# Means and variances of tiles 12 to 15 by ScalarE's accumulators instead of VectorE's statistics

## The chip, the cores and the metric

The kernel runs on one core of one Trainium2 chip. The metric is the time of one execution in device microseconds. The engines are TensorE (PE; its weight loads are PEld), VectorE (DVE), ScalarE (ACT) and GpSimd (POOL). SyncE (SP) issues most of the loads and stores.

## The reference

Two layers, each of an attention block and a gated feed-forward block, both behind a layer norm without weights. The sequence has 2048 rows of 448; there are 16 query heads of 28, and one key and one value head that all share.

```python
def _layernorm(x, axis=-1, eps=1e-5):
    m = jnp.mean(x, axis=axis, keepdims=True)
    v = jnp.var(x, axis=axis, keepdims=True)
    return (x - m) / jnp.sqrt(v + eps)
...
        q = (lambda x, *d: x.transpose(*d))((x @ wq).reshape(B, S, H, Dh), 0, 2, 1, 3)
        k = x @ wk
        v = x @ wv
        scores = jnp.einsum("bhqd,bkd->bhqk", q, k) * (Dh ** -0.5)
        p = _softmax(scores, axis=-1)
        o = jnp.einsum("bhqk,bkd->bhqd", p, v)
...
        g = jnp.einsum("bsd,df->bsf", x, w_gate)
        u = jnp.einsum("bsd,df->bsf", x, w_up)
        h = _sigmoid(g) * u
        return jnp.einsum("bsf,fd->bsd", h, w_down)

    x = A_x
    x = x + _A_ref(_layernorm(x, axis=-1), A_wq, A_wk, A_wv, A_wo)
    x = x + _B_ref(_layernorm(x, axis=-1), B_w_gate, B_w_up, B_w_down)
    x = x + _A_ref(_layernorm(x, axis=-1), A_wq, A_wk, A_wv, A_wo)
    x = x + _B_ref(_layernorm(x, axis=-1), B_w_gate, B_w_up, B_w_down)
```

## The kernel before

The 2048 rows are 16 tiles of 128 rows. Each number that TensorE multiplies is split into two float16 parts, a high one and a low one, and a product of two is three matmuls. Ahead of the main loop stands a prologue of some 90 us. In it each tile of x is loaded (`load_x0`, L900), gets its mean and variance, is normalised (L947 on ScalarE, L949 on VectorE), is cast to its high part (L953), has its low part made (two rows, L958 and L959, on VectorE or GpSimd), is transposed by TensorE in seven pieces (L335) and copied out of PSUM into XT (L337). From XT come the tile's keys and values (`kv`, L352, copied out in the rows L379, L380 and L381) and, by four tiles, the queries (qp, also L352, copied out in L406 and L409). As soon as keys and queries are there, TensorE forms score blocks only for the row maxima (mx, L549), which VectorE reduces (mp, L554). The main loop that follows computes scores (s, L584), their exponentials (L587) and the products with the values (pv, L595), with the feed-forward matmuls in between.

The order of the prologue is written out by hand as the string `SEQ`: each word is a step and its arguments, and the steps are issued in that order, so that on every engine the instructions stand in the order of the words. Some steps defer an instruction until the next step that flushes. `h,n` gives n matmuls on the identity (hot, L916) whose result nobody reads. The words that matter here:

- `s,a,z,how`: statistics of tiles a to z−1 on VectorE, one `bn_stats` (L924) and one `bn_aggr` (L925) a tile. With how = 1 or 2 the reciprocal root follows on GpSimd (`rstd`, eight short rows from L306 to L314 with how = 2)
- `n`, `g`, `l`, `t`, `k`, `c`: norm, high part, low part, transposes, keys, and the transposed keys of one tile
- `qs,c`: square sum of one quarter of the query weights on ScalarE (L109), `qw,c,how`: its split into high and low part (L126 or L135 on ScalarE, then L127 on VectorE, or L136 and L137 on GpSimd)

The step `s,12,16,2` stands behind `k,8`. The tiles' loads are all issued by SP at the start, tiles 12 to 15 last, and each load of SP's queue takes the next of eight semaphores (DMAHW0 to DMAHW7), so it is issued only once the load eight places ahead of it has landed. Buffers of the accumulating passes and of the squares, junx and junq, are three slots in rotation.

Of the kernel before, what the change touches and what calls it, by code (L numbers as in the profile page):

```python
# [8 lines left out]
F32 = mybir.dt.float32  # L9
F16 = mybir.dt.float16  # L10
I32 = mybir.dt.int32
AF = mybir.ActivationFunctionType
OP = mybir.AluOpType
# [6 lines left out]
def interleaved_layers_kernel(ctx: ExitStack, tc: tile.TileContext, x, wq, wk, wv, wo, wg, wu, wd, out, layers=2):  # L20
# [6 lines left out]
    nc = tc.nc  # L27
    _, S, D = x.shape
# [13 lines left out]
    wk1 = ctx.enter_context(tc.tile_pool(name="wk1", bufs=2))  # L42
# [105 lines left out]
    def prep_kv():  # L148
        junk = wk1.tile([128, 4, Dh], F32, tag="xr", name="junk", bufs=4)
        squares(mxa[:, 0:1], rkv[:, 0], junk)  # L150
        squares(mxa[:, 1:2], rkv[:, 1], junk)
        yield from scales(mxa[:, 0:2], 2, pwa[:, 0:2], swa[:, 0:2])
        for i in range(2):
            split(WKV[:, 0, :, i * Dh:(i + 1) * Dh], WKV[:, 1, :, i * Dh:(i + 1) * Dh], rkv[:, i], swa[:, i:i + 1])
# [149 lines left out]
    def rstd(mv, r, n, bias=False):  # L304
        v, y, z, w = (r[:, k, :n] for k in range(4))
        nc.gpsimd.tensor_scalar(v, mv[:, :n, 1], EPS, None, op0=OP.add)  # L306
        nc.gpsimd.tensor_tensor(y, v, mhalf[:, :n], op=OP.pow)
        nc.gpsimd.tensor_tensor(z, y, y, op=OP.mult)
        nc.gpsimd.tensor_tensor(z, z, v, op=OP.mult)
        nc.gpsimd.tensor_scalar(z, z, -1024.0, 3072.0, op0=OP.mult, op1=OP.add)  # L310
        nc.gpsimd.tensor_tensor(w, y, z, op=OP.mult)
        if bias:
            nc.gpsimd.tensor_scalar(z, mv[:, :n, 0], -1.0, None, op0=OP.mult)
            nc.gpsimd.tensor_tensor(z, z, w, op=OP.mult)  # L314
            return [(z[:, i:i + 1], w[:, i:i + 1]) for i in range(n)]
        return [(mv[:, i, 0:1], w[:, i:i + 1]) for i in range(n)]
# [576 lines left out]
    xr0 = {}  # L893
# [8 lines left out]
    hl0, ls0 = {}, {}  # L902
# [69 lines left out]
            pass  # L972
        kv_done(0)

    raw0 = {}
    pkv = prep_kv()
    parts = wk1.tile([128, 4], F32, name="parts", bufs=1)
    pws = scales(mxa[:, 2:3], 1, pwa[:, 2:3], swa[:, 2:3])
# [24 lines left out]
    def first_mx():  # L1003
        nonlocal nmx
        flush()
        while QDONE.get((0, 0), 0) <= nmx % G and QDONE.get((0, 0), 0) < G:
# [1 line left out]
        mxs[0].step()  # L1008
        nmx += 1

    DO = {"s": stats, "r": refine, "n": norm, "g": high, "l": low, "t": turn, "k": keys, "c": keyst, "m": first_mx,
          "h": heat, "a": lambda: next(pkv, None), "qs": qsq, "qx": qsum, "qy": lambda: next(pws), "qw": qsplit,
          "q": queries, "f": lambda a: fill.slice(a * QCH / 100), "p": advance, "e": flush}
    SEQ = (
# [13 lines left out]
    )  # L1028
    for o in SEQ.split():
        a = o.split(",")  # L1030
        DO[a[0]](*map(int, a[1:]))
    for b in range(1, NB):
# [26 lines left out]
    for l in range(layers):  # L1059
# [8 lines left out]
        else:  # L1068
            mx.todo.sort()
            n = sum(a[0] < 4 for a in mx.todo) + 4  # L1070
# [10 lines left out]
        for step in range(U * KT):  # L1081
# [6 lines left out]
            for o in pair[kt % 2]:  # L1088
                if o == "S":
                    scores(l, u, kt, len(P), P)  # L1090
                elif o == "M":
                    if l and step < 3 * KT:
                        n = step in sparse
                    else:
                        n = 1 + (u == 0 and kt in MORE)
                    if not n:
                        mx.visit()
                    for _ in range(n):
                        if not mx.step() and not final and l + 1 in mxs:
                            a = mxs[l + 1].between()  # L1100
# [28 lines left out]
        n = 0  # L1129
        nx = None if final else mxs[l + 1]  # L1130
        while side or pend or (fill.gens if final else not nx.started()):
# [4 lines left out]
            a = None if final else nx.between()  # L1136
            if a:
# [7 lines left out]
                if go:  # L1145
                    nx.step(a)
                    n = 0
# [25 lines left out]
```

## Time and profile before

| what | value |
|---|---|
| median of 3 runs | 2244.06 us (2243.4 to 2244.54) |
| the profiled execution | 2247.71 us |
| its span | 2245.9 us |
| TensorE busy, share of the span | 2195.5 us, 98% |
| VectorE busy | 1643.7 us, 73% |
| ScalarE busy | 1552.8 us, 69% |
| GpSimd busy | 335.9 us, 15% |
| mean granted TensorE clock | 0.995 |

The three runs are without a profile; the profiled execution is one more, and every duration below comes from it. Busy shares are means over the whole span, and a prologue of 90 us is 4% of it, so they say nothing on who waits for whom there; for that the timelines of the engines are read.

### The profile page before, as it was taken

The page shows a single profiled execution, that of the slowest core. Times are in us where ns is not written, and L with a number is a line of the kernel's source. Part 1 is how long each engine was busy: PE and PEld are TensorE (multiplying, and loading weights), DVE is VectorE, ACT ScalarE, POOL GpSimd, SP SyncE. Part 2 cuts the span into 40 slices and gives each one's busy share as a digit, 9 for nine tenths or more (in the row PEclk, how much of TensorE's full clock was granted, in tenths as well). Part 3 has the DMA queues.
Part 4 walks back from the last instruction along what each step waited for, and adds up shares of the span by engine and source line. Part 5 has one row for each costly group of instructions (what it writes and reads, how often), then busy time and mean ns, then how long its engine had stood idle before and what let it go on. Part 6 is the DMA issues. An engine that isn't in the chain of part 4 may idle for free.

```text
span 2245.9 us, 41454 instructions
## 1 busy us (share of the span) xinstructions
PE 2195.5 (98%) x15915; PEld 1030.8 (46%) x15915; DVE 1643.7 (73%) x2905; ACT 1552.8 (69%) x2595; POOL 335.9 (15%) x590
## 2 busy tenths in 40 slices
PE   7998999999999999999999999999999999999999
PEld 3322344444544445454564324445454544445467
DVE  7888888777777787777796557777777777777222
ACT  5698777776667677676614997777676767777741
POOL 5113764101010100101012010000000000000010
PEclk9999999999999999999999999999999999999999
DMA  4333662323313232331441113323231313223233
GB/s 143 106 97 94 197 215 81 106 79 85 112 60 102 64 100 90 97 107 49 119 154 35 36 52 108 80 88 99 67 108 49 100 59 103 76 88 96 75 118 108
DMA packets 203622, 213.28 MB, mean 95 GB/s; under 512 B 135376, under 2 KB 164240, under 8 KB 203424
## 3 DMA queue, kind: packets, MB, share of 16 engines
q1 hardware_dynamic: 198080, 195.78, 29.2%
q0 software_dynamic: 5344, 14.87, 1.9%
q8 instruction: 124, 2.03, 0.4%
q14 instruction: 74, 0.61, 0.1%
HBM read 175.37 MB, written 23.59 MB: 89 GB/s over the span
## 4 chain that ended last, share of the span: by engine, by line
PE 86%; DVE 8%; ACT 2%; issue 1%; DMA 1%; SPq 1%; POOL 0%; DVEq 0%; ACTq 0%; POOLq 0%
PE pv L595 20%; PE s L584 19%; PE up L352 11%; PE dn L784 11%; PE gp L352 11%; PE mx L549 7%; DVE mp L554 6%; PE wo L695 3%; PE qp L352 2%; ACT P L587 1%; DMA wgu<-wgu_d 0%; DMA rq<-in_A_wq_dram 0%; DMA rc<-sums 0%; PE hot L916 0%; DVE sgu L131 0%
## 5 line engine op out<-in xcount | busy, mean ns | idle before, releaser
L587 ACT ACTIVATE P<-s,esc 128x512 f32<-128x512 f32 x2048 | 1297.8, 690 | 474.5 <-PE s L584 462.8
L554 DVE TENSOR_REDUCE mp<-mx 128x1 f32<-128x512 f32 x2048 | 1269.4, 682 | 389.2 <-PE mx L549 385.4
L584 PE MATMUL s<-QS,KK 96*128 96x512 f16 x2048 | 673.8, 381 | 21.3 <-DVE mp L554 14.8
L352 PEld LDWEIGHTS <-wgu 128*128 128x128 f16 x4928 | 467.6, 97 | 182.1 <-issue 42.9
L595 PE MATMUL pv<-P,VV 128*32 128x512 f32 x4096 | 510.7, 602 | 0.0
L352 PE MATMUL gp<-XT,wgu 128*128 128x256 f16 x2464 | 349.2, 272 | 2.4 <-DVE mp L554 1.7
L352 PE MATMUL up<-XT,wgu 128*128 128x256 f16 x2464 | 348.3, 272 | 0.7 <-DVE mp L554 0.7
L784 PE MATMUL dn<-WD,h 128*128 128x448 f16 x1344 | 301.0, 352 | 0.0
L584 PEld LDWEIGHTS <-KK 96*128 96x128 f16 x2048 | 189.7, 97 | 212.5 <-issue 114.5
L595 PEld LDWEIGHTS pv<-P,VV 128*32 128x32 f32 x4096 | 98.7, 108 | 244.6 <-issue 242.6
L549 PE MATMUL mx<-KK,QH 32*128 32x512 f16 x1792 | 185.3, 386 | 3.0 <-DVE mp L554 1.7
L784 PEld LDWEIGHTS <-h 128*128 128x128 f16 x1344 | 126.5, 97 | 129.4 <-issue 14.5
L549 PEld LDWEIGHTS <-QH 32*128 32x128 f16 x1792 | 46.0, 91 | 256.5 <-issue 252.7
L669 POOL TENSOR_TENSOR lb<-pvs,lb 128x512 f32<-128x512 f32 x32 | 41.1, 1284 | 739.1 <-DMA lb<-sums 619.8
L757 ACT ACTIVATE h<-th 128x512 f16<-128x512 f32 x112 | 70.3, 628 | 61.8 <-DVE th L754 61.5
L754 DVE SCALAR_TENSOR_TENSOR th<-th,up 128x512 f32<-128x512 f32 x112 | 76.2, 680 | 48.9 <-PE up L352 42.2
L306 POOL TENSOR_SCALAR rs<-mv 128x1 f32<-128x1 f32 (+1 forms) x50 | 11.2, 225 | 656.6 <-DVE mv L291 573.6
L352 PE MATMUL qp<-XT,WQ 128*128 128x512 f16 x352 | 108.3, 390 | 0.7 <-DVE mp L554 0.4
L746 ACT ACTIVATE th<-gp,gsc 128x512 f32<-128x512 f32 x112 | 76.8, 685 | 32.8 <-PE gp L352 32.6
L758 DVE SCALAR_TENSOR_TENSOR h<-th,h 128x512 f16<-128x512 f32 x112 | 79.9, 713 | 20.8 <-ACT h L757 20.8
L695 PE MATMUL wo<-WO,oT 128*128 128x448 f16 x384 | 89.7, 352 | 0.2 <-ACT P L587 0.2
L352 PEld LDWEIGHTS <-WQ 128*128 128x128 f16 x352 | 32.9, 99 | 54.9 <-issue 28.9
(151 smaller groups left out, 918.1 us busy)
## 6 DMA issues: line engine op xcount, KB each, us to landing
wgu<-wgu_d SPq DMA_DIRECT2D x224, 512.0 KB
QS<-qd SPq DMA_DIRECT2D x384, 32.0 KB
lb<-sums SPq DMA_DIRECT2D x128, 64.0 KB
xr<-in_A_x_dram SPq DMA_DIRECT2D x32, 224.0 KB
qd<-qst POOLq DMA_DIRECT2D x28, 256.0 KB, 2.7
wgu_d<-sgu POOLq DMA_DIRECT2D x14, 512.0 KB, 3.7
x2d<-x SPq DMA_DIRECT2D x16, 224.0 KB
xr<-x2d SPq DMA_DIRECT2D x16, 224.0 KB
```

Source lines behind the costliest of these rows:

```text
L352: nc.tensor.matmul(ps, a, b, start=n == 0, stop=n == 10)
L549: nc.tensor.matmul(ps[h][:, i * w:(i + 1) * w], qh[32 * h:32 * h + 32, g], KK[l][32 * h:32 * h + 32, 1, ka:kz], start=True, stop=True, til ...
L554: nc.vector.tensor_reduce(o, ps[h].rearrange("p (g k) -> p g k", g=n), axis=AX.X, op=OP.max)
L584: nc.tensor.matmul(s, KK[l][0:96, 0, kt * 128:(kt + 1) * 128], QS[l, u][:, g].rearrange("p h n -> p (h n)"), start=True, stop=True)
L587: nc.scalar.activation(p, s, AF.Exp, scale=esc)
L595: nc.tensor.matmul(v[32 * g:32 * g + 32], VV[l][:, kt], P[g], start=kt == 0, stop=kt == KT - 1, tile_position=(0, 32 * g))
L695: nc.tensor.matmul(p, v["oT"][:, a, h * 128:(h + 1) * 128], WO[:, c, h], start=n == 0, stop=n == 11)
L746: defer(lambda: nc.scalar.activation(th, gp.rearrange("p j n -> p (j n)"), AF.Tanh, scale=gsc))
L754: nc.vector.scalar_tensor_tensor(t, th, 1.0, up.rearrange("p j n -> p (j n)"), op0=OP.add, op1=OP.mult)
L757: nc.scalar.activation(h[:, 0], t, AF.Copy, scale=2.0 ** -17)
L758: defer(lambda: nc.vector.scalar_tensor_tensor(h[:, 1], t, 2.0 ** -17, h[:, 0], op0=OP.mult, op1=OP.subtract), 3)
L784: nc.tensor.matmul(p, hs[f // 2][:, a, o:o + 128], WD[:, f, c], start=n == 0, stop=n == 3 * FC - 1)
```

## The change

The words `s,12,16,2` leave `SEQ`, and with them VectorE's four pairs of statistics and one `rstd` chain on GpSimd. In their place stand four words `x,i` (`total`): ScalarE passes over the raw tile and accumulates its sum, and GpSimd multiplies the sum by −1/448. Four words `y,i` (`spread_of`): ScalarE squares the tile with that negative mean as its bias and accumulates the squares. And one word `z,12` (`settle`): GpSimd forms mean and variance of the four tiles from the sums and runs the same `rstd` chain. The new words are dealt between the steps of the first four keys, `z` behind the second pass of tile 15.

```diff
-    raw0 = {}
+    def sm_of(i):
+        a = i // 4 * 4
+        if a not in sm0:
+            sm0[a] = wk1.tile([128, 3, 4], F32, name="sm", bufs=2)
+        return [sm0[a][:, k, i - a:i - a + 1] for k in range(3)]
+
+    def total(i):
+        sm = sm_of(i)
+        junk = wk1.tile([128, D], F32, tag="s2", name="junx", bufs=3)
+        nc.scalar.activation(junk, xr0[i], AF.Identity, accum_out=sm[0])
+        nc.gpsimd.tensor_scalar(sm[1], sm[0], -1.0 / D, None, op0=OP.mult)
+
+    def spread_of(i):
+        sm = sm_of(i)
+        junk = wk1.tile([128, D], F32, tag="s2", name="junx", bufs=3)
+        nc.scalar.activation(junk, xr0[i], AF.Square, bias=sm[1], accum_out=sm[2])
+
+    def settle(a):
+        mv = wk1.tile([128, 4, 2], F32, name="mv", bufs=4)
+        r = wk1.tile([128, 4, 4], F32, name="rs", bufs=4)
+        sm = sm0[a]
+        nc.gpsimd.tensor_scalar(mv[:, :, 0], sm[:, 1], -1.0, None, op0=OP.mult)
+        nc.gpsimd.tensor_scalar(mv[:, :, 1], sm[:, 2], 1.0 / D, None, op0=OP.mult)
+        for j, t in enumerate(rstd(mv, r, 4, True)):
+            ls0[a + j] = t
+
+    sm0, raw0 = {}, {}
...
-        "qs,2 h,2 qs,1 n,2,0 a e g,3,0 t,0,0 l,3,0 t,1,0 qs,0 g,2,0 h,2 l,2,1 k,0 h,3 s,4,8,1 h,5 t,2,1 qx qy "
-        "k,1 c,0,0 k,2 e t,3,1 c,1,0 n,4,0 h,1 qw,0,0 h,5 n,6,0 qw,1,1 h,2 k,3 n,5,0 qw,2,0 h,1 g,4,0 h,2 "
...
-        "s,12,16,2 g,10,0 t,9,0 f,75 c,7,0 m h,2 m n,11,1 h,1 h,3 k,9 l,10,1 n,12,1 h,1 t,10,0 g,11,0 f,110 "
...
+        "qs,2 h,2 qs,1 n,2,0 a e g,3,0 t,0,0 l,3,0 t,1,0 x,12 qs,0 g,2,0 h,2 l,2,1 k,0 x,13 h,3 s,4,8,1 h,5 "
+        "t,2,1 qx qy k,1 c,0,0 x,14 k,2 x,15 e t,3,1 c,1,0 y,12 n,4,0 h,1 qw,0,0 h,5 n,6,0 qw,1,1 h,2 k,3 "
+        "y,13 n,5,0 qw,2,0 h,1 g,4,0 h,2 l,4,0 qw,3,1 g,5,0 y,14 q f,50 l,5,0 t,4,0 c,2,1 y,15 z,12 c,3,1 "
```

On ScalarE, around the square of the last quarter of the query weights (junq) and the first key (ktl, VV), the queue differs so. The tiles are xr_159, 161, 163 and 165 for 12 to 15; in brackets stands whom a row waits for.

```order
 L337 COPY XT_121<-t_258 128x7x128 [waits PE_49]
+L984 ACTIVATE junx,sm<-xr_159 128x448 [waits DMAHW2_49,Activation_49]
 L109 ACTIVATE junq,parts<-rq 128x448 [waits Activation_49]
-L953 CAST hl_279<-xr_136 128x448 [waits DVE_49]
+L953 CAST hl_283<-xr_136 128x448 [waits DVE_49]
 L337 COPY XT_121<-t_269 128x7x128 [waits PE_49]
+L984 ACTIVATE junx,sm<-xr_161 128x448 [waits DMAHW3_49,Activation_49]
 L379 ACTIVATE ktl_111<-kv 128x7x28 [waits PE_49]
 L380 ACTIVATE VV<-kv 128x28
```

Tile 12's total stands ahead of that square and waits for its load, and tile 13's ahead of the first key. The cast is the same on both sides but for a buffer's number.

Some 2 us further in the same queue, from the first transposed keys (KK) to the splits of the query weights (WQ):

```order
 L379 ACTIVATE ktl_112<-kv 128x7x28 [waits PE_49]
 L380 ACTIVATE VV<-kv 128x28
+L984 ACTIVATE junx,sm<-xr_163 128x448 [waits DMAHW4_49,Activation_49]
 L392 COPY KK<-kvt 128x2x128 [waits PE_49]
+L984 ACTIVATE junx,sm<-xr_165 128x448 [waits DMAHW5_49,Activation_49]
 L379 ACTIVATE ktl_111<-kv 128x7x28 [waits DVE_49,PE_49]
 L380 ACTIVATE VV<-kv 128x28
+L990 ACTIVATE junx,sm<-xr_159,sm 128x448 [waits Pool_49]
 L126 ACTIVATE WQ<-rq,swa 128x16x28 [waits DVE_49]
 L135 ACTIVATE WQ<-rq,swa 128x16x28
 L392 COPY KK<-kvt 128x2x128 [waits PE_49]
+L990 ACTIVATE junx,sm<-xr_161,sm 128x448 [waits Activation_49,Pool_49]
```

The totals of tiles 14 and 15 stand ahead of the third key, the square of tile 12 ahead of the first two splits of the query weights, and that of tile 13 ahead of the two that follow.

On SP nothing moves. These are its loads of tiles 6 to 15, xr_147 to xr_165, as they stand in both kernels:

```order
L900 DMA xr_147<-in_A_x_dram 128x448 [waits DMAHW4_49]
L900 DMA xr_149<-in_A_x_dram 128x448 [waits DMAHW5_49]
L900 DMA xr_151<-in_A_x_dram 128x448 [waits DMAHW6_49]
L900 DMA xr_153<-in_A_x_dram 128x448 [waits DMAHW7_49]
L900 DMA xr_155<-in_A_x_dram 128x448 [waits DMAHW0_49]
L900 DMA xr_157<-in_A_x_dram 128x448 [waits DMAHW1_49]
L900 DMA xr_159<-in_A_x_dram 128x448 [waits DMAHW2_49]
L900 DMA xr_161<-in_A_x_dram 128x448 [waits DMAHW3_49]
L900 DMA xr_163<-in_A_x_dram 128x448 [waits DMAHW4_49]
L900 DMA xr_165<-in_A_x_dram 128x448 [waits DMAHW5_49]
```

The load of tile 14 waits for the semaphore that tile 6's load counts up, and that of tile 15 for tile 7's. What is new is who reads tiles 12 to 15 first: ScalarE, at the start, where it was VectorE, behind `k,8`.

## Rows read from the trace of the kernel before

**Rows 1.** The page: the span, and the shares by line of the chain that ended last.

```profile
span 2245.9 us, 41454 instructions
...
PE pv L595 20%; PE s L584 19%; PE up L352 11%; PE dn L784 11%; PE gp L352 11%; PE mx L549 7%; DVE mp L554 6%; PE wo L695 3%; PE qp L352 2%; ACT P L587 1%; DMA wgu<-wgu_d 0%; DMA rq<-in_A_wq_dram 0%; DMA rc<-sums 0%; PE hot L916 0%; DVE sgu L131 0%
```

**Rows 2.** Timeline, SP's queue: start us, us, engine, line, operation, out<-in.

```profile
7.25 0.44 SPq L900 DMA_DIRECT2D xr<-in_A_x_dram  x1
...
12.94 0.43 SPq L900 DMA_DIRECT2D xr<-in_A_x_dram  x1
...
13.99 0.33 SPq L900 DMA_DIRECT2D xr<-in_A_x_dram  x1
...
14.58 0.33 SPq L900 DMA_DIRECT2D xr<-in_A_x_dram  x1
```

**Rows 3.** Timeline, ScalarE, 15 to 24 us; in brackets idle us before.

```profile
15.98 0.57 ACT L109 ACTIVATE junq<-rq 128x448 f32<-128x448 f32 x1
...
16.55 0.55 ACT L953 CAST hl<-xr 128x448 f16<-128x448 f32 x1
...
18.03 0.18 ACT L380 ACTIVATE VV<-kv 128x28 f32<-128x28 f32 x1
...
19.88 0.33 ACT L379 ACTIVATE ktl<-kv 128x196 f16<-128x196 f32 x1 [1.67 <-PE kv L352]
...
20.73 0.70 ACT L126 ACTIVATE WQ<-rq,swa 128x448 f16<-128x448 f32 x1
...
23.14 0.70 ACT L135 ACTIVATE WQ<-rq,swa 128x448 f16<-128x448 f32 x1
```

**Rows 4.** Timeline, VectorE, 18.8 to 28.6 us.

```profile
18.86 0.17 DVE L381 SCALAR_TENSOR_TENSOR ktl<-kv,ktl 128x28 f16<-128x28 f32 x1
...
21.98 0.68 DVE L127 SCALAR_TENSOR_TENSOR WQ<-rq,swa,WQ 128x448 f16<-128x448 f32 x1
...
26.78 0.19 DVE L381 SCALAR_TENSOR_TENSOR ktl<-kv,ktl 128x28 f16<-128x28 f32 x1
...
27.02 1.43 DVE L959 TENSOR_TENSOR hl<-xr,hl 128x384 f16<-128x384 f32 x1
```

**Rows 5.** Timeline, TensorE's matmuls, 13 to 100 us.

```profile
28.50 0.50 PE L335 MATMUL t<-id,hl 128*128 128x128 f16 x3 [0.96 <-DVE hl L959]
...
33.45 0.56 PE L335 MATMUL t<-id,hl 128*128 128x128 f16 x7
...
49.44 0.50 PE L335 MATMUL t<-id,hl 128*128 128x128 f16 x3 [0.64 <-POOL hl L959]
...
56.67 0.42 PE L549 MATMUL mx<-KK,QH 32*128 32x512 f16 x4
```

**Rows 6.** Groups by line, ScalarE, 0 to 60 us: busy us, mean ns.

```profile
L947 ACT ACTIVATE xr<-xr,rs 128x448 f32<-128x448 f32 x7 | 5.4, 765 | 2.4 <-POOL rs L314 2.4
```

**Rows 7.** Timeline, VectorE, 45 to 51 us.

```profile
45.05 0.62 DVE L924 BATCH_NORM_STATS2 st<-xr 128x6 f32<-128x448 f32 x1
...
48.65 0.19 DVE L381 SCALAR_TENSOR_TENSOR ktl<-kv,ktl 128x28 f16<-128x28 f32 x1 [0.57 <-ACT VV L380]
...
50.73 0.69 DVE L554 TENSOR_REDUCE mp<-mx 128x1 f32<-128x512 f32 x1 [1.90 <-PE mx L549]
```

**Rows 8.** Timeline, GpSimd, 18 to 100 us.

```profile
30.70 0.44 POOL L958 TENSOR_TENSOR hl<-xr,hl 128x64 f16<-128x64 f32 x1 [2.67 <-DVE hl L953]
...
49.47 0.23 POOL L306 TENSOR_SCALAR rs<-mv 128x4 f32<-128x4 f32 x1
...
52.34 0.20 POOL L314 TENSOR_TENSOR rs<-rs 128x4 f32<-128x4 f32 x1
```

**Rows 9.** Windows: PE, PEld, DVE, ACT, POOL busy us (instructions); granted clock, DMA share, GB/s.

```profile
28.40:31.70 3.30, 3.20 (x20) 1.72 (x21) 1.98 (x7) 0.43 (x3) 1.00 (x2) 0.50 0.00 0
...
48.90:55.60 6.70, 6.16 (x39) 2.88 (x40) 4.87 (x9) 3.47 (x7) 4.17 (x12) 0.50 0.91 295
...
57.00:91.00 34.00, 31.25 (x247) 13.47 (x244) 33.42 (x66) 22.12 (x49) 3.48 (x6) 1.00 0.29 91
```

More of the change, by code (lines that the diff above doesn't have):

```diff
@@ L1009, in first_mx @@
         nmx += 1
-    DO = {"s": stats, "r": refine, "n": norm, "g": high, "l": low, "t": turn, "k": keys, "c": keyst, "m": first_mx,
+    DO = {"s": stats, "r": refine, "x": total, "y": spread_of, "z": settle, "n": norm, "g": high, "l": low, "t": turn, "k": keys, "c": keyst, "m": first_mx,
           "h": heat, "a": lambda: next(pkv, None), "qs": qsq, "qx": qsum, "qy": lambda: next(pws), "qw": qsplit,
```

18 rows, old and new, of the table SEQ are left out of this document.

## Prediction

> **What bounds the kernel now.** I read the page first: TensorE's pv and s lines, 20% and 19%, lead the chain that ended last [rows 1], so the loop behind the prologue is TensorE's. Whatever the prologue's last step is late by, the loop starts late by, and nothing in the change touches the loop. So I asked of the first 60 us alone which engine works without a gap, and where the edited places lie in that.
>
> From 18.86 to 28.45 us VectorE runs on without a wait, from the small key row (L381) to the low half of tile 5 (L959) [rows 4], and TensorE waits 0.96 us for that last row before it transposes tile 5 at 28.50 [rows 5]. From there the chain is TensorE's query products, VectorE's maxima and statistics of tiles 8 to 11, and GpSimd's queue up to 49.4 us, where TensorE waits 0.64 us for GpSimd's L959 [rows 5]. From 48.9 to 55.6 us TensorE is busy 6.16 of 6.70 us at a granted clock of 0.50 (1.2 GHz). From 57 to 91 us VectorE is busy 33.42 of 34.00 us: the maxima [rows 9].
>
> **What is taken away.** VectorE's four pairs of statistics start at 45.05 us. The next row, L381 at 48.65, has waited 0.57 us for ScalarE, so the four pairs end at 48.08 and cost 48.08 − 45.05 = 3.03 us. But behind them VectorE waits: those 0.57 us, and then 1.90 us for TensorE's mx before 50.73 [rows 7]. TensorE's mx there stands behind the transposes of tile 9, which wait for GpSimd and not for VectorE. Without the statistics VectorE's wait grows by 3.03 us and the reduction at 50.73 starts when it did. Worth: 0.
>
> GpSimd's rstd chain for these tiles runs from 49.47 to 52.34 + 0.20 = 52.54 us [rows 8], 3.07 us. The low half of tile 10 moves up by that. TensorE, which would use it, transposes tile 10 only after hot and kv matmuls without a wait, at half clock; the mx at 56.67 follows with no wait ahead of it either [rows 5]. Worth: 0. If either of these covers were gone, 3.03 us would be the most to win; that is a rival below.
>
> **What is added, and where it is queued.** ScalarE gets eight passes. The total is like the square at 15.98 us: with its accumulator read the next instruction starts at 16.55, so 0.57 us each [rows 3]. The trace has no square whose bias is a pointer to a column. Below, it is the 0.57 us of the same square; above, a 128x448 pass with both scale and bias by pointer has a mean of 765 ns [rows 6], against 0.57 for the square's own row: 0.57 + 0.20 = 0.77. With one pointer I take the middle, 0.67 us, since the copy with a pointer as its scale at 20.73 took 0.70 [rows 3], 0.13 over the square.
>
> The Trainium skill, "ScalarE: Activation LUTs", section "What ACT_TABLE_LOAD costs", puts each pointer operand at about 93 ns; by it the pass would be 0.66 and the sum 0.01 us smaller.
>
> **The first wait is new: the load of tile 12.** In before nothing reads tile 12 until 45 us. Now its total stands in ScalarE's queue ahead of the square of the query weights, and waits for the tile's load (semaphore DMAHW2). Behind it in ScalarE's queue are that square, the cast of tile 2, the eviction of tile 1's transposes and the first key, and VectorE, GpSimd and TensorE wait for these.
>
> When does tile 12 land? Its load is issued at 12.94 us [rows 2]. SP's queue reuses eight semaphores, so the load of tile 14 waits until that of tile 6 has landed, and that of tile 15 until that of tile 7; both start after a gap, at 13.99 and 14.58 us. So tile 6, issued at 7.25, needed 6.7 us, and tiles land 14.58 − 13.99 = 0.59 us apart [rows 2]. Five tiles after tile 7 is tile 12: 14.58 + 5 x 0.59 = 17.53 us. ScalarE is there at 15.98 us [rows 3]: it stands 1.55 us. Below: nothing, if the load were in by 15.98; above: 12.94 + 6.74 = 19.68 us, tile 6's own time in flight, a stall of 3.70. I take 17.53, the pace of the very queue. Tiles 13 to 15 follow at 18.1, 18.7 and 19.3, ahead of their passes by the times below.
>
> **The sum, step by step.**
> 1. The stall and tile 12's pass put the square, the cast and the eviction 1.55 + 0.57 = 2.12 us later; tile 13's pass makes it 2.69 for the first key. Its last row, 18.03 + 0.18 = 18.21 us, ends at 20.90. VectorE took it up at 18.86 [rows 4]; now at 20.95, so 2.09 later. Of ScalarE's 2.69 the 0.65 us of slack on VectorE are gone.
> 2. The second key waits for TensorE, which waits for VectorE: 19.88 becomes 21.97. ScalarE's old wait there, 1.67 us, covers tile 13's pass, not the stall.
> 3. From 19.88 to 20.73 ScalarE had no gap [rows 3]. Tiles 14 and 15 and the square of tile 12 now stand before the query weights: 0.57 + 0.57 + 0.67 = 1.81. The split at 20.73 starts at 20.73 + 2.09 + 1.81 = 24.63 and ends, 0.70 later, at 25.33.
> 4. VectorE's part of that split (L127) started at 21.98, though ScalarE's had ended at 21.43. Now it starts at 25.33 + 0.05 = 25.38: 3.40 us later.
> 5. From 21.98 to 28.45 VectorE has no wait, 6.47 us. The square of tile 13 puts ScalarE's later split 0.67 behind that, and VectorE comes to it just as it is done; the squares of tiles 14 and 15 stand behind the last cast that this stretch of VectorE needs, but for one key row, and ScalarE has that ready in time: 23.14 + 3.90 + 0.67, the splits' shift and tile 13's square, puts the last split's start at 27.71, and cast, square and key row after it end before 29.9, where VectorE takes the key at 26.78 + 3.40 = 30.18. So tile 5's low half ends at 31.85, and TensorE's transposes start 3.4 us late.
> 6. The new rstd chain on GpSimd, 3.07 us with two short rows more, some 3.6, now stands ahead of tile 6's low half, which GpSimd began at 30.70 after a wait of 2.67 [rows 8]. TensorE takes that tile at 33.45 without a wait. With everything 3.4 later, the chain ends at about 35.6, the low half at 36.9, TensorE needs it at 36.85: hidden to within 0.1. If GpSimd starts later still, the excess adds to the sum one for one at most.
>
> From 32 us on every engine does what it did, 3.4 us later. **Sum: +3.4 us.** The profiled execution, 2247.71 us (its span 2245.9 and 1.8 around it), would become 2251.1. It stands 3.65 us above the median of the runs, so on the runs' scale it is 2244.06 + 3.4 = 2247.5 us, 0.15% more. Differences up to 0.2%, 4.5 us, are about what a measurement of this kernel can't tell from no change.
>
> **Rivals.**
> *The load is in time.* The stall is 0. The first key then ends at 18.21 + 1.14 = 19.35 and VectorE starts it 0.54 late; the three passes of step 3 put L127 at 21.98 + (0.54 + 1.81 − 0.50), where 0.50 is its old slack: +1.85, so 2245.9. For it speaks that an idle queue lands a tile fast; against it that tile 6 took 6.7 us in this queue [rows 2]. The Trainium skill, "DMA: Bandwidth & Descriptors", section "Anatomy of one DMA", gives about 2.0 us plus bytes over 436 GB/s, an estimate of 2.5 us for 224 KB, fitted on the other kind of queue; by it tile 12 would be in at about 15.5, which is this rival. The trace disagrees for tile 6.
>
> *The clock costs a stretch more.* TensorE's new gaps, 2 to 3 us between 18 and 32, come ahead of work at full clock. After the gaps at 25 to 28 us it ran the 28.40 to 31.70 stretch at 0.50, where it was busy 3.20 us [rows 9]; at half clock such a stretch loses 1.6 us. One more of them on the path, or tile 12 landing 1.6 us later, and it is 2244.06 + 5.0 = 2249.1. Against it: the old half-clock stretch at 28.4 moves along with the transposes, so a second need not come.
>
> *Faster.* VectorE bounds 57 to 91 us [rows 9], and it is rid of 3.03 us just before. If the maxima at 50.73 could start earlier by that, and ScalarE's passes lay in its waits, it would be 2241.0. It decides if TensorE reaches its mx 3 us sooner; for that GpSimd's queue before 49.44 would have to be shorter, and nothing is taken from it there. Only the half-clock stretch from 48.9, if it fell away with the new timing, would give the like, about 3 us.
>
> *No effect.* All eight passes fall into ScalarE's waits and the load is early: 2244.1. Against it is step 3: ScalarE has no gap there.
>
> **How the numbers follow.** Forecast, +3.4: 0.57, with 2246.5 to 2248.6 its own range. Load in time: 0.14. A stretch more: 0.18. Faster: 0.06. No effect: 0.05. From 2243.5 to 2250.0 the range holds all but the faster case and the upper part of the stretch, some 0.15. Slower by over 0.2% means above 2248.55: most of the stretch case and a tenth of the forecast, 0.21. Faster by over 0.2%, below 2239.6, needs the faster case and a clock stretch besides: 0.03. The rest, 0.76, is within 0.2%.
>
> **What would show it.** In the profile after, ScalarE's row L984 for tile 12 starts at about 17.5 us behind a wait for the load of x, the first key's rows end near 20.9, L127 on VectorE starts near 25.4, and the transposes of tile 5 near 31.9. VectorE's wait for mx near 50 us (then 54) is longer by the 3 us it was rid of. I am wrong if L984 starts at 16.0 with no wait, if L127 waits for something other than ScalarE, or if the stretch from 32 to 60 us gives back or adds more than 1 us.

## The result and the profile after

The changed kernel took 2251.39 us (median of 6 runs, 2248.53 to 2254.53), the kernel before 2244.51 us beside it (6 runs, 2243.4 to 2248.47; three of them are those of the table before): ratio 1.0025, 95% interval 1.0014 to 1.0037. Timed again in another job it took 2249.17 us (11 runs) against 2246.59 (27 runs): 1.0015, 1.0006 to 1.0024. Single executions of either kernel lie up to 6.4 us from their median, so sizes of 1 us are read below from traces, not from times. It is slower, by 3.4 us at the second ratio and 5.6 at the first (the medians lie 2.6 and 6.9 us apart); the predicted 2247.5 us and its range, which ended at 2250.0, lie under the first timing; the second lies within that range.

The page of the kernel after answers to [rows 1]: the span is 3.9 us longer than that of the execution on which the prediction rests, and the shares of the chain are the same.

```profile
span 2249.8 us, 41475 instructions
...
PE pv L595 20%; PE s L584 19%; PE dn L784 11%; PE up L352 11%; PE gp L352 11%; PE mx L549 7%; DVE mp L554 6%; PE wo L695 3%; PE qp L352 2%; ACT P L587 1%; DMA xr<-in_A_x_dram 0%; DVE sgu L131 0%; PE kv L352 0%; DMA rc<-sums 0%; PE hot L916 0%
```

New in the chain is the load of x (xr). ScalarE's timeline shows where it stands; it answers to [rows 3].

```profile
17.45 0.58 ACT L984 ACTIVATE junx<-xr 128x448 f32<-128x448 f32 x1 [1.67 <-DMA xr<-in_A_x_dram]
...
20.62 0.18 ACT L380 ACTIVATE VV<-kv 128x28 f32<-128x28 f32 x1
...
24.07 0.69 ACT L990 ACTIVATE junx<-xr,sm 128x448 f32<-128x448 f32 x1
24.72 0.69 ACT L126 ACTIVATE WQ<-rq,swa 128x448 f16<-128x448 f32 x1
```

Tile 12's total waits 1.67 us for its load and starts at 17.45. The square of the query weights (junq) follows at 18.02, the first key's last row ends at 20.80, and the square about the mean takes 24.72 − 24.07 = 0.65 us. On VectorE, which answers to [rows 4], the small key row (20.84) and L127 (25.44) come when the prediction had them (20.95 and 25.38), but tile 5's low half (the last row) does not:

```profile
25.44 0.69 DVE L127 SCALAR_TENSOR_TENSOR WQ<-rq,swa,WQ 128x448 f16<-128x448 f32 x1
...
28.08 1.07 DVE L958 TENSOR_TENSOR hl<-xr,hl 128x64 f16<-128x64 f32 x1
29.07 0.57 DVE L959 TENSOR_TENSOR hl<-xr,hl 128x384 f16<-128x384 f32 x1
...
30.02 0.21 DVE L958 TENSOR_TENSOR hl<-xr,hl 128x64 f16<-128x64 f32 x1
30.15 0.55 DVE L959 TENSOR_TENSOR hl<-xr,hl 128x384 f16<-128x384 f32 x1
```

It ends at 30.70 where 31.85 was forecast: 2.25 us late, not 3.40. GpSimd's queue, which answers to [rows 8], holds the opposite surprise. The first two rows are parts of the query weights' split, 32.07 to 36.12 is the new chain (two of its ten rows stand here), and behind it comes tile 6's low half:

```profile
27.85 1.22 POOL L137 TENSOR_TENSOR WQ<-rq,WQ 128x448 f16<-128x448 f32 x1
29.06 1.79 POOL L136 TENSOR_SCALAR rq<-rq,swa 128x448 f32<-128x448 f32 x1
...
32.07 0.48 POOL L996 TENSOR_SCALAR mv<-sm 128x4 f32<-128x4 f32 x1
...
35.92 0.20 POOL L314 TENSOR_TENSOR rs<-rs 128x4 f32<-128x4 f32 x1
36.07 0.30 POOL L958 TENSOR_TENSOR hl<-xr,hl 128x64 f16<-128x64 f32 x1
```

TensorE's matmuls, which answer to [rows 5], wait for that half twice, at tile 6:

```profile
31.34 2.54 PE L352 MATMUL qp<-XT,WQ 128*128 128x512 f16 x11
...
36.43 0.23 PE L335 MATMUL t<-id,hl 128*128 128x128 f16 x1 [1.84 <-POOL hl L958]
37.30 0.34 PE L335 MATMUL t<-id,hl 128*128 128x128 f16 x3 [0.64 <-POOL hl L959]
...
57.21 0.76 PE L549 MATMUL mx<-KK,QH 32*128 32x512 f16 x4
...
96.28 1.94 PE L595 MATMUL pv<-P,VV 128*32 128x512 f32 x8
...
103.14 1.12 PE L595 MATMUL pv<-P,VV 128*32 128x512 f32 x8
```

Tile 6, taken at 33.45 us in before, is done with its last part from 37.30 on, and yet the maxima at 57.21 are only 0.54 us behind those at 56.67 in before. The windows show why; they answer to [rows 9] (granted clock third from the right):

```profile
21.40:24.80 3.40, 3.40 (x38) 2.59 (x38) 1.77 (x10) 2.70 (x12) 2.06 (x7) 0.50 0.02 5
...
38.50:41.90 3.40, 3.40 (x10) 1.21 (x9) 2.83 (x9) 1.94 (x6) 1.18 (x2) 0.50 0.24 80
...
93.10:103.30 10.20, 9.42 (x31) 2.15 (x34) 4.81 (x9) 6.01 (x11) 0.84 (x1) 0.50 0.66 220
```

The stretch of before at a granted clock of 0.50 from 48.9 to 55.6 us is not there in this execution. Instead TensorE runs at half clock (1.2 GHz) from 21.4 us on for 3.4 us, just behind the wait for tile 6, and for 10.2 us from 93.1. So the stages don't simply move: the half-clock stretches stand elsewhere. All traces below are read at one mark, the second group of eight pv matmuls (L595), which comes behind the stretch near 93 us or at its end: 103.14 us here. What the stretches ahead of it cost is still in the mark; the last table sets their sum beside it. The first profile of before has it at 99.66:

```profile
94.67 1.94 PE L595 MATMUL pv<-P,VV 128*32 128x512 f32 x8
...
99.66 1.06 PE L595 MATMUL pv<-P,VV 128*32 128x512 f32 x8
```

VectorE near 50 us answers to [rows 7]:

```profile
52.82 0.19 DVE L381 SCALAR_TENSOR_TENSOR ktl<-kv,ktl 128x28 f16<-128x28 f32 x1 [2.37 <-ACT VV L380]
53.24 4.88 DVE L554 TENSOR_REDUCE mp<-mx 128x1 f32<-128x512 f32 x8 [0.24 <-PE mx L549]
```

The 3.03 us of statistics are gone, and VectorE still waits, 2.37 and 0.24 us; before had 0.57 and 1.90.

### The profile page after: what moved, and what is told of

It is laid out like the page before. It is cut to its first block, busy times and chain, and to the rows that moved or that the text cites. A ratio compares the mean times of both kernels' runs of the same rounds, so it can differ in the third digit from the quotient of the medians.

```text
span 2249.8 us, 41475 instructions
## 1 busy us (share of the span) xinstructions
PE 2198.8 (98%) x15915; PEld 1031.3 (46%) x15915; DVE 1638.0 (73%) x2897; ACT 1559.3 (69%) x2611; POOL 339.1 (15%) x596
## 4 chain that ended last, share of the span: by engine, by line
PE 86%; DVE 8%; ACT 2%; issue 2%; DMA 1%; POOL 1%; SPq 0%; ACTq 0%; DVEq 0%; POOLq 0%
PE pv L595 20%; PE s L584 19%; PE dn L784 11%; PE up L352 11%; PE gp L352 11%; PE mx L549 7%; DVE mp L554 6%; PE wo L695 3%; PE qp L352 2%; ACT P L587 1%; DMA xr<-in_A_x_dram 0%; DVE sgu L131 0%; PE kv L352 0%; DMA rc<-sums 0%; PE hot L916 0%
## 5 line engine op out<-in xcount | busy, mean ns | idle before, releaser
L595 PE MATMUL pv<-P,VV 128*32 128x512 f32 x4096 | 510.8, 602 | 0.0
L595 PEld LDWEIGHTS pv<-P,VV 128*32 128x32 f32 x4096 | 98.7, 109 | 244.9 <-issue 242.9
```

The costliest lines, as they stand in the source:

```text
L595: nc.tensor.matmul(v[32 * g:32 * g + 32], VV[l][:, kt], P[g], start=kt == 0, stop=kt == KT - 1, tile_position=(0, 32 * g))
```

## The experiments

Four theories are tried. A: two places cost, the totals ahead of the first keys (a wait for the load, and the passes) and GpSimd's new chain ahead of tile 6's low half. B: eight passes cost ScalarE's time wherever they stand. C: VectorE bounds, so taking its statistics away should have won something, and what was won hides a larger loss. D: the change is slower because TensorE's half-clock stretches fall otherwise. The edits to the order of the program are shown as pieces of SEQ. Each time is a median, its ratio taken against the kernel before in the same job: 2244.92 us in the job of the first four kernels, 2246.59 in that of the second four, 2245.01 in that of the last.

**Is taking the statistics away worth anything?** The kernel before without the four pairs of statistics and without GpSimd's rstd chain for them; tiles 12 to 15 are normalized with the columns of tiles 8 to 11, so that part of the computation is left out.

```diff
-k,8 s,12,16,2 g,10,0
+k,8 g,10,0
...
-bias=ls0[i][0], scale=ls0[i][1])
+bias=ls0[i - i // 12 * 4][0], scale=ls0[i - i // 12 * 4][1])
```

> The kernel before without the statistics of tiles 12 to 15 at all: VectorE's four pairs and GpSimd's root chain are gone, nothing stands in their place, and tiles 12 to 15 are normalised with the columns of tiles 8 to 11, so part of the computation is left out. Theory A (the prologue's schedule: VectorE waits behind these statistics anyway, so they were worth nothing): VectorE's wait before the maxima near 50.7 us grows by 3 us, the last maxima of the prologue start within 0.3 us of where they did, and the time is that of before, 2244.5 us within 1.5. Theory C (VectorE bounds the prologue, so the 3 us come off): 2241.5 us. GpSimd's 3.07 us less make the low half of tile 10 earlier; A expects nothing from that either.

Measured: 2246.12 us, ratio 1.0005 (0.9996 to 1.0014). Nothing was to be won there, on VectorE or GpSimd: C falls. The trace shows why, and just as the prediction had it. VectorE's waits ahead of the maxima grow from 0.57 + 1.90 us to 3.51 + 1.89, that is by 2.93 of the 3.03 us that it was rid of:

```profile
50.37 0.19 DVE L381 SCALAR_TENSOR_TENSOR ktl<-kv,ktl 128x28 f16<-128x28 f32 x1 [3.51 <-ACT VV L380]
52.45 4.88 DVE L554 TENSOR_REDUCE mp<-mx 128x1 f32<-128x512 f32 x8 [1.89 <-PE mx L549]
```

These maxima start 1.72 us later than before's at 50.73, and the mark comes 1.71 us later. Tile 6, ahead of the edit, is already late by as much (35.17 us against 33.45), behind a half-clock stretch at 16.4 us that before's first profile doesn't have.

```profile
101.37 1.06 PE L595 MATMUL pv<-P,VV 128*32 128x512 f32 x8
```

**The rstd chain behind tile 8's keys.** The changed kernel with one word of the sequence moved:

```diff
-y,15 z,12 c,3,1
+y,15 c,3,1
...
-k,8 g,10,0
+k,8 z,12 g,10,0
```

> The changed kernel with one word moved: z,12 (GpSimd's root chain for tiles 12 to 15) from behind the second pass of tile 15 to the place behind k,8 where the statistics of these tiles stood before. Theory A (what the early passes cost is mostly absorbed by 34 us; the chain ahead of tile 6's low half then makes TensorE wait 1.84 + 0.64 us): both waits are gone, TensorE's transposes of tile 6 start at about 34.3 us and end there, the statistics of tiles 8 to 11 start at about 36.8 instead of 39.0, and the time falls by 1 to 3 us, to 2248.5 to 2250.5. Theory B (the cost is ScalarE's eight passes themselves, wherever the chain stands): 2251.4, unchanged.

Measured: 2248.92 us, 1.002 (1.0011 to 1.0029). TensorE now takes tile 6 without a wait, at 34.19 us and no longer from 36.43 to 37.30:

```profile
34.19 0.56 PE L335 MATMUL t<-id,hl 128*128 128x128 f16 x7
```

The wait is gone, but the time doesn't show it. The first pv group starts at 94.75 us, beside before's 94.67; then this execution too has a half-clock stretch of 10.2 us, from 91.8, in which that group lies, and the second group starts at 101.61.

```profile
91.80:102.00 10.20, 9.22 (x31) 2.18 (x33) 4.58 (x9) 6.01 (x12) 0.79 (x1) 0.50 0.66 217
```

**The first two totals behind the first key and the transposes of tile 2.**

```diff
-t,1,0 x,12 qs,0 g,2,0 h,2 l,2,1 k,0 x,13 h,3
+t,1,0 qs,0 g,2,0 h,2 l,2,1 k,0 h,3
...
-t,2,1 qx qy k,1
+t,2,1 x,12 x,13 qx qy k,1
```

> The changed kernel with the totals of tiles 12 and 13 moved behind the first key (x,12 and x,13 behind t,2,1), where ScalarE waited 1.67 us in before; all else as in the changed kernel. Theory A: no wait for the load of tile 12 (or under 0.1 us), the first key's rows end at about 18.2 as in before, VectorE's L127 starts at 23.6 to 23.9 instead of 25.4, and GpSimd's root chain begins about 1.5 us earlier, so TensorE's wait for tile 6's low half shrinks from 2.5 us to about 1; time 2249 to 2250.5. Theory B: the same eight passes, 2251.4. If the wait for the load were the whole of the loss, 2246 or less.

Measured: 2247.3 us, 1.001 (1.0001 to 1.0018). ScalarE's timeline has no wait for a load, and the split starts 2.50 us earlier than after the change (24.72):

```profile
17.79 0.57 ACT L984 ACTIVATE junx<-xr 128x448 f32<-128x448 f32 x1
...
22.22 0.65 ACT L126 ACTIVATE WQ<-rq,swa 128x448 f16<-128x448 f32 x1
```

The 2247.3 us are under the 2249 to 2250.5 that theory A expected. At tile 6 TensorE still waits for the low half behind the chain, though less:

```profile
34.67 0.34 PE L335 MATMUL t<-id,hl 128*128 128x128 f16 x3 [0.64 <-POOL hl L959]
```

Its first pv group starts at 95.02 us, its second at 99.99, 0.33 us behind that of before's first profile, whose half-clock stretches stand alike. So either move takes its wait out of the trace; what each is worth in time, ratios whose intervals overlap don't tell.

**All passes in ScalarE's waits from 32 to 42 us**, the rstd chain behind tile 8's keys:

```diff
-x,12 x,13 x,14 x,15 y,12 y,13 y,14 y,15 z,12
...
+l,6,1 e x,12 x,13 c,4,1
+f,50 m x,14 x,15 y,12 y,13 f,40 h,2
+e f,10 y,14 y,15 n,8,1
+k,8 z,12 g,10,0
```

> All eight passes moved out of the first keys into ScalarE's waits between 32 and 42 us (totals of tiles 12 and 13 ahead of the transposes of tile 6, the other totals and the squares of 12 and 13 ahead of the key of tile 6, the last two squares ahead of the norm of tile 8), and GpSimd's root chain back behind k,8. Theory A: nothing up to 32 us differs from before, no pass delays another engine by more than 0.5 us, VectorE's 3 us are gone and change nothing; time that of before, 2244.5 within 1.5. Theory B (the passes cost wherever they stand): 2248 or more. Theory C (VectorE bounds): 2241.5.

Measured: 2248.65 us, 1.0016 (1.0007 to 1.0025). Theory A expected the time of before, so this is a miss; by the time alone the passes cost wherever they stand. The trace shows a place that the edit made itself. The square of tile 14, which stands ahead of tile 8's norm on ScalarE, waits 3.11 us for GpSimd to scale that tile's sum (L985), and GpSimd comes to it only behind the rstd chain of tiles 8 to 11. TensorE then waits 1.94 us for tile 8:

```profile
41.70 0.39 POOL L985 TENSOR_SCALAR sm<-sm 128x1 f32<-128x1 f32 x2
```

```profile
41.95 0.67 ACT L990 ACTIVATE junx<-xr,sm 128x448 f32<-128x448 f32 x1 [3.11 <-POOL sm L985]
```

```profile
44.67 0.61 PE L335 MATMUL t<-id,hl 128*128 128x128 f16 x4 [1.94 <-ACT hl L953]
```

Its first pv group starts at 94.43 us. That is level with before's first profile (94.67), but 1.83 us behind the second (92.60), which like this execution has no half-clock stretch at 28.4 us. A half-clock stretch of 10.2 us (from 91.1) then makes the second group late. No run has the passes late without that wait, so how the 3.7 us divide is open.

```profile
94.43 1.93 PE L595 MATMUL pv<-P,VV 128*32 128x512 f32 x8
...
101.28 1.09 PE L595 MATMUL pv<-P,VV 128*32 128x512 f32 x8
```

**Both moves together**: the edits of the second and third experiments.

```diff
-t,1,0 x,12 qs,0
+t,1,0 qs,0
...
-k,0 x,13 h,3
+k,0 h,3
...
+t,2,1 x,12 x,13 qx qy k,1
...
-y,15 z,12 c,3,1
+y,15 c,3,1
...
+k,8 z,12 g,10,0
```

> The change with both moves: the totals of tiles 12 and 13 behind the transposes of tile 2, and the rstd chain behind the keys of tile 8. Theory A (two places cost, and nothing else does): the wait for tile 12's load and the late low half of tile 6 are both gone, so TensorE's transposes of tile 6 start within 0.5 us of before's 33.45 us and the time is within 2 us of the kernel before, 2244 to 2247 us, ratio 0.9995 to 1.001. Theory B (the eight passes cost wherever they stand, about 0.5 us each): still 3 to 4 us over before, 2248 to 2249 us, as each of the two moves alone. Theory D (what is left is TensorE's half clock behind 91 us): the time goes by the length of the half-clock stretch there: with 3.4 us at the level of before, with 10.2 us some 2 us over it.

Measured: 2246.45 us, 1.0005 (0.9996 to 1.0014). What is left of the slowdown can't be told from no change, with all eight passes still on ScalarE: the 3 to 4 us of B are not there, and A's two places hold together. TensorE takes tile 6 at 32.52 us, and the second pv group starts ahead of that in before's first profile:

```profile
98.60 1.06 PE L595 MATMUL pv<-P,VV 128*32 128x512 f32 x8
```

**Other executions of the two kernels.** No edit.

> The kernel before, profiled in another execution. Theory D: the program is the same, and yet at least one of its half-clock stretches stands elsewhere or has another length than in the first profile (28.4, 48.9, 93.2, 130.8, 1219.6 us), and the span differs from 2245.9 us by 1 us or more with it. The rival, that the clock follows the program and the spread comes from elsewhere (DMA, measuring): the same stretches to 0.5 us, and a span within 1 us or a difference with no change of the clock.

Measured: one run, 2247.09 us. The half-clock stretch at 28.4 us, in which tile 5's query products ran in before's first profile [rows 9], is not there:

```profile
28.40:31.70 3.30, 3.30 (x32) 1.66 (x29) 2.04 (x6) 1.50 (x4) 1.92 (x3) 1.00 0.12 40
```

Its tile 6 comes at 31.35 us, not at 33.45, with the same program, and so does the mark:

```profile
97.20 1.06 PE L595 MATMUL pv<-P,VV 128*32 128x512 f32 x8
```

It loses that gain again behind 1220 us, so its span is 2245.3 us, 0.6 from the first. Both sides were right in part: the stretches move, the span hardly did.

> The changed kernel, timed once more and profiled in another execution. Theory A: the wait for tile 12's load (1.67 us before the total at 17.45) and the low half of tile 6 at 36.07 us stand as in the first profile, since the program sets them; the time is 5 to 7 us over before. Theory D: the half-clock stretches (21.4, 38.5, 93.1 of 10.2 us, 134.0, 1222.9 us) are not all where they were, and the span moves with them by 1 us or more. If the span is the same to 0.5 us with the stretches unchanged, the clock follows the program here.

Measured: 2249.17 us, 1.0015 (1.0006 to 1.0024), less than the 5 to 7 us over before that theory A expected. The wait for the load stands again (1.51 us ahead of 17.38), but TensorE's first wait at tile 6 is 0.17 us instead of 1.84: the query products ahead of it ran at half clock from 31.1 to 34.5 us. Its matmuls' rows, and the window of that stretch:

```profile
36.51 0.23 PE L335 MATMUL t<-id,hl 128*128 128x128 f16 x1 [0.17 <-POOL hl L958]
37.38 0.34 PE L335 MATMUL t<-id,hl 128*128 128x128 f16 x3 [0.64 <-POOL hl L959]
...
102.64 1.06 PE L595 MATMUL pv<-P,VV 128*32 128x512 f32 x8
```

```profile
31.10:34.50 3.40, 3.40 (x21) 1.55 (x19) 1.67 (x5) 1.56 (x6) 3.03 (x5) 0.51 0.00 0
```

The tile is done at the same time in both executions: the low half sets it. And the stretch near 93 is 3.4 us here, not 10.2.

**Hot matmuls in TensorE's waits near 90 us.** Two matmuls on the identity, results unused, behind each of the first four score tiles; first in the kernel before, twice, and then in the changed kernel.

```diff
                 if o == "S":
                     scores(l, u, kt, len(P), P)
+                    if not l and not step:
+                        heat(2)
```

> The kernel before with two hot matmuls (results unused) behind each score tile of the first step of layer 0, in TensorE's waits near 89 to 93 us. Theory D: TensorE does not rest there, so the half-clock stretch at 93.2 us is gone or shorter, and the time falls by 1 to 2 us: 2243 to 2244 us, ratio 0.9992 to 0.9997. Rival: the stretch costs nothing that the rest doesn't hide, or the hot matmuls take as much as they save: within 0.5 us of before, or slower by their own time, about 1 us.

Measured: 2241.44 us, 0.9983 (0.9974 to 0.9992). Ahead of its stretch at 93 the kernel before waits for VectorE between its first scores, longest in this row of its first profile, and runs the 16 us around it at a mean clock of 0.89:

```profile
92.00 0.39 PE L549 MATMUL mx<-KK,QH 32*128 32x512 f16 x2 [0.52 <-DVE qst L416]
```

```profile
88.00:104.00 16.00, 13.58 (x66) 3.77 (x64) 11.37 (x24) 11.85 (x21) 0.84 (x1) 0.89 0.49 157
```

With the hot matmuls the same 16 us have the full clock, and the mark is at 94.78:

```profile
88.00:104.00 16.00, 15.36 (x91) 4.42 (x89) 13.78 (x32) 14.40 (x26) 1.53 (x2) 1.00 0.43 147
```

```profile
94.78 1.06 PE L595 MATMUL pv<-P,VV 128*32 128x512 f32 x8
```

The stretch at 130.8 is gone as well, which I had not counted in; with these hot matmuls it is absent in three of five executions, and one of 3.4 us stands near 125 or 128 us in the other two.

> The kernel before with the hot matmuls behind the first scores, timed and profiled a second time beside the three kernels below. Theory D: again without half-clock stretches at 93 and 130 us, and again 3 to 5 us under before: ratio 0.998 to 0.9987. Rival, that the first time was a lucky job: within 2 us of before.

Measured: 2241.89 us, 0.9984 (0.9975 to 0.9992): it holds. The mark is at 96.19.

```profile
96.19 1.06 PE L595 MATMUL pv<-P,VV 128*32 128x512 f32 x8
```

> The changed kernel with the same hot matmuls. They take the half-clock stretches behind 91 us out of the comparison, which differed between the executions (10.2 us and 3.4 us long). Theory A: the lateness of the prologue is left whole, some 3 us: 3 to 4 us over the kernel before with the hot matmuls, which makes 2244 to 2246 us, ratio to before 0.9995 to 1.0003. Theory D alone (the change is slower because its half-clock stretch is longer): within 1 us of the kernel before with the hot matmuls, 2241 to 2243 us.

Measured: 2245.03 us, 1.0003 (0.9994 to 1.0011), which is 3.1 us over the same edit in the kernel before, run in the same job (4.3 us by the two ratios). With the stretches near 93 and 130 us gone from both profiles, the change's cost is still there, and so it is at the mark:

```profile
99.07 1.07 PE L595 MATMUL pv<-P,VV 128*32 128x512 f32 x8
```

> The change with both moves and with the hot matmuls: passes on ScalarE behind the first key, rstd chain behind the keys of tile 8. Theory A: both places are mended, so it is level with the kernel before with the hot matmuls, 2240.5 to 2243 us, ratio 0.998 to 0.9988. Theory B (passes cost wherever they stand): 2 to 4 us over it. If removing VectorE's statistics were worth something, it would be 1 us or more under it.

Measured: 2242.98 us, 0.9991 (0.9982 to 1.0), a little over the 0.998 to 0.9988 that theory A expected. It lies over before with hot matmuls by 1.1 us in the medians and 1.7 in the means; the two intervals overlap, but a rest of 1 to 2 us is not excluded. It isn't lost in the prologue: at the mark it is level with the first of those two, and its span is 1.8 us longer than that of the second (2240.0 against 2238.2):

```profile
94.70 1.06 PE L595 MATMUL pv<-P,VV 128*32 128x512 f32 x8
```

**Hot matmuls at the border of the layers too**, in the kernel before:

```diff
-    def heat(n):
+    def heat(n, h=None):
+        h = hot if h is None else h
...
+        if l:
+            hot1 = psv.tile([128, 512], F32, tag="v", name="hot")
+            heat(11, hot1)
         while late:
...
         fill.slice((0.50 if l else 0.4) * QCH)
+        if l:
+            heat(4, hot1)
...
                     scores(l, u, kt, len(P), P)
+                    if not step:
+                        heat(2, hot1 if l else hot)
```

> The kernel before with hot matmuls also at the border of the layers: eleven in TensorE's wait of 3 us for VectorE's row maxima there, four ahead of the first scores, and two behind each score tile of the first step of layer 1. Theory D: the half-clock stretch of 3.4 to 6.8 us at 1216 to 1223 us goes, worth 1.5 to 2 us more than the hot matmuls of layer 0 alone: 2239 to 2241 us, ratio 0.9973 to 0.998. Rival: something else bounds the border (the exponentials on ScalarE, the load of the query scales), and the hot matmuls bring nothing or 0.5 to 1 us more of their own.

Measured: 2241.46 us, 0.9985 (0.9975 to 0.9995), level with the hot matmuls of layer 0 alone. Half clock at the border is gone (granted clock 1.00 from 1208 to 1228 us), TensorE's wait of 3.05 us there is down to 0.56, and it brought nothing: the 1.5 to 2 us more that I expected were wrong.

```profile
1208.00:1228.00 20.00, 18.70 (x137) 7.48 (x136) 9.77 (x19) 12.52 (x24) 6.18 (x7) 1.00 0.18 56
```

Up to the mark this is the same program as the two before it, and a third profile of it:

```profile
97.43 1.07 PE L595 MATMUL pv<-P,VV 128*32 128x512 f32 x8
```

## Why the prediction was wrong

The mark, the second pv group, collects what the prologue lost. Beside it stands how long TensorE ran at half clock between 13 us and the mark, added up from the trace; several values are several profiles.

| kernel | at half clock, us | mark, us |
|---|---|---|
| before | 13.7; 10.2 | 99.66; 97.20 |
| before, no statistics | 17.1 | 101.37 |
| before, hot matmuls | 3.4; 6.8; 10.2 | 94.78; 96.19; 97.43 |
| after | 16.9; 17.1 | 103.14; 102.64 |
| after, hot matmuls | 6.8 | 99.07 |
| after, chain moved | 20.0 | 101.61 |
| after, first totals moved | 13.7 | 99.99 |
| all passes late | 17.0 | 101.28 |
| after, both moves | 13.7 | 98.60 |
| after, both moves, hot matmuls | 6.8 | 94.70 |

In the six executions of the kernel before the mark rises with the half clock ahead of it, by about half of it: from 94.78 at 3.4 us to 101.37 at 17.1. Set against the execution of it with as much half clock, the changed kernel is 1.3 to 1.8 us later without hot matmuls and 2.9 with them. That says too little, since its first stretch, from 21 to 23 us on, lay off the path (see below): with that one left out of its sum it is 3.0 to 3.5 us later, and 4.3 with hot matmuls. Against the second profile of before it is up to 5.9 us later, and there half clock is part of the difference. With both moves it is 1.1 and 1.5 us earlier than before at like sums.

**Steps 1 to 4 held.** Load (17.45 for 17.53), first key (20.80 for 20.90), second key (22.10 for 21.97), split (24.72 for 24.63) and L127 (25.44 for 25.38) came within 0.13 us of the forecast. The pace of the kernel's own queue had the load to 0.1 us: the tile came at 17.45. The Trainium skill, "DMA: Bandwidth & Descriptors", section "Anatomy of one DMA", whose figures are fitted on the other kind of queue, led to an estimate of 15.5 us; for this filled queue it is not borne out. For the pass with one pointer, the Trainium skill's "ScalarE: Activation LUTs", section "What ACT_TABLE_LOAD costs", led to 0.66 us; the trace has 0.65.

**Step 5 was mis-sized.** It took VectorE's 6.47 us as fixed; they became 30.70 − 25.44 = 5.26 us, and 3.46 late became 2.25. Rows with two inputs change their length with what GpSimd does beside them. In before, L959 at 27.02 took 1.43 us [rows 4] while GpSimd's L137 ran:

```profile
26.98 1.05 POOL L137 TENSOR_TENSOR WQ<-rq,WQ 128x448 f16<-128x448 f32 x1
```

After the change, L137 ran from 27.85 to 29.07, the tiny L958 at 28.08 took 1.07 us and ended 0.08 us behind it, and both L959 took 0.57 and 0.55. The Trainium skill, "SBUF — State Buffer", section "SBUF: two separate sides", says that a VectorE operation with two inputs from SBUF and a GpSimd operation that reads SBUF exclude each other for a whole instruction. For L137 the trace agrees; it doesn't for L136, which has one tensor input: beside it, from 29.06 to 30.85 us, both L959 ran in 0.57 and 0.55 us. L136 is not without effect, though: in the profile of before an L959 at 25.64 took 0.90 us beside it, and why is open.

**Step 6 failed.** It held the rstd chain hidden "to within 0.1" behind TensorE's arrival at tile 6, 36.85 us. GpSimd's side of that was nearly right: tile 6's low half ended at 36.33 + 0.91 = 37.24 for 36.9, though the chain, with its two short rows, took 36.12 − 32.07 = 4.05 us, not 3.6. The cover was wrong. TensorE stood ready for that half at 36.43 − 1.84 = 34.59 us, 1.15 us sooner by step 5, and 1.2 us sooner because its query products ahead of tile 6 no longer ran at half clock (eleven took 2.54 us). In before's first profile the same eleven were in the stretch from 28.4:

```profile
29.34 3.74 PE L352 MATMUL qp<-XT,WQ 128*128 128x512 f16 x11
```

The price is 1.84 + 0.64 us in one execution and 0.17 + 0.64 behind a half-clock stretch in the other. "The excess adds to the sum one for one" was right, and I gave it no size. So GpSimd's queue, and no longer VectorE's low half of tile 5, sets when tile 6 is done: at 37.64 us, 3.63 behind before's 34.01. That this is near the forecast 3.4 is luck: 1.15 us too much at step 5 made up for the wait that was left out.

**"From 32 us on every engine does what it did" failed too.** The second execution of the changed kernel comes near it (span 2249.4 against 2245.9: +3.5), the first doesn't. The second rival, a half-clock stretch more behind TensorE's new gaps, named 2249.1 us and is the nearest of the cases. Such a stretch is there: from 20.1 to 22.6 us on, TensorE falls to half clock in all four profiles that keep the totals ahead of the first key, and there in none of the ten others. But it lay off the path: in the first execution the second key came within 0.13 us of the forecast and L127 within 0.06. What cost time in the first execution was another, 10.2 us at half clock in place of 3.4 near 93 us. From the first pv group to the second it is 6.86 us in that execution (96.28 to 103.14), 4.99 in before. But it can't be the whole: the changed kernel with hot matmuls, without half clock there, is still 3.1 us over its counterpart.

**The base was too low and too lucky.** The sum was set on 2244.06 us, a median of three runs; later jobs gave 2244.9, 2246.6 and 2245.0. On the scale of profiled executions the forecast was 2251.1 us, and the changed kernel's took 2251.58; the median of the runs missed by 3.9 us. To come from one scale to the other, 3.65 us had been taken off, the distance of one execution of before from the median of three. From the later medians that execution lies 1.1 to 2.8 us. And the sum was worked out in one execution, whose half-clock stretch at 28.4 was taken for a property of the program; a second execution doesn't have it.

**The zeros held**, and without the statistics and their chain as told: the ratio is 1.0005, and the waits grew by 2.93 us. In the changed kernel VectorE's waits before the maxima at 53.24 did not grow by 3 us: they are 2.37 + 0.24 = 2.61 us, for 0.57 + 1.90 = 2.47 in before [rows 7]. VectorE came to that stage later, and what it was rid of went into catching up to the same wait for TensorE's mx. So the rival "faster" is refuted, "no effect" as well, and "load in time" by the 1.67 us.

D alone is not enough, then, nor is A alone for the whole of the first timing. Shown: the totals ahead of the first key and the chain ahead of tile 6's low half together bring most of the lateness. With both moved, the median falls by 2.72 us in one job, where it lay 2.58 over before, and with hot matmuls by 2.05 of 3.14 us in another. How much each place costs by itself is read from the traces alone. Open: the rest of 1 to 2 us with hot matmuls, and how often the stretch near 93 us is 10.2 us long. The changed kernel had it in one of two profiles, the variants with only the chain moved and with all passes late in their one, and the kernel before in none of two; with so few executions I can't say that the change makes it likelier, nor how the first timing's 5.6 us and the second's 3.4 divide.

## What to carry to other kernels

Moving work to an engine that is idle on average is paid at the place in its queue: ask what stands behind it, whether its input has landed by then, and how much slack each of those rows has. The late passes paid this once more, 3.11 us behind another chain. A term that is "hidden to within 0.1" is not hidden; give it a price, and look whether the cover is a stretch at half clock, since such a stretch need not come in the next execution. Profile the kernel before twice before working out sums of a few us, and where TensorE has waits shortly ahead of a stretch at half clock, a few matmuls with unused results in them are worth trying: eight gave 0.9983 here, about as much as the change cost.

## What I had not expected of the hardware

The stretches at half clock stand at other places in two executions of one program (28.4 us in one profile of before, none there in the other), and one near 93 us was 3.4 or 10.2 us long in the same kernel. Eight hot matmuls in TensorE's own waits took away the stretch at 93 us in five executions, and that near 130 us in three of them. Fifteen and eight more at the border of the layers took one away there as well, without any gain. A VectorE row of 128x64 took 1.07 us beside GpSimd's two-input L137 and 0.21 beside L136, with one.
